# Last output rows in 384 and 128 columns, middle tiles stored in two parts, last load of w_out in two: a two-layer kernel on one core

## The chip, the core and the metric

One core of a Trainium2 chip. The metric is device time in microseconds (us), the median over several executions. All executions here were fast (granted TensorE clock 0.997 to 1.000). A profile is one of these executions; its span is some 2.1 us shorter than the device time of the same execution (285.6 against 287.74 for the kernel before).

## The reference, cut to what matters

```python
kv  = einsum('bhsd,bhse->bhde', k, v)            # 8 batches, 8 heads, 576 rows, 64 wide
out = einsum('bhsd,bhde->bhse', q, kv)
x   = out / sqrt(mean(out*out) + 1e-6) * g_norm  # -> 4608 rows of 512
h   = x @ w_in                                   # 512 -> 2048
y   = (h * sigmoid(1.702 * h)) @ w_out           # 2048 -> 512
```

The kernel works in nine tiles of 512 rows: tiles 0 to 7 hold the first 512 rows of a batch each, tile 8 the 64 rows left over of each of the eight. A tile has a first layer (`hT`, 64 matmuls of 512 columns) and a second layer (`o`, 64 more); the attention of the next batch is woven in between. Step n of a second layer is its n-th matmul, counted from 0.

## The kernel before: the parts that matter

```python
LAST = ((0, DM // 2), (DM // 2, DM))          # DM = 512: two parts of 256 columns

def project_last(mo):                          # tile 8, its last 128 rows
    for i, (n0, n1) in enumerate(LAST):
        o = ps_a.tile([P, n1 - n0], F32, name="oh", tag="att")
        for fo in range(FO):                   # FO = 16 blocks of w_out
            nc.tensor.matmul(o, gT[:, fo, mo * P : (mo + 1) * P],
                             w_out_sb[:, fo, n0:n1], ...)
        copy = nc.vector.tensor_copy if i else nc.scalar.copy
        copy(osb[:, mo, n0:n1], o)
        store_rest(mo, n0, n1)                 # 64 rows on SP's queue, 64 on ACT's

# second layer of tile 0 ("deep"): four passes over four blocks of w_out each
steps = [(mo, 4 * i + k) for i in range(4) for mo in range(4) for k in range(4)]

# loads of w_out, issued by POOL among those of k and v of batch 1
load_w_out(0, 4) ... load_w_out(4, 8)
for c in (0, 2):
    load_half("k", 1, c, c + 2)
    load_half("v", 1, c, c + 2)
    load_w_out(8 + 2 * c, 12 + 2 * c)          # blocks 8-11, then 12-15

# tiles 2 to 7: one store of 1 MB at the end of the tile
nc.sync.dma_start(out=out[t * S : t * S + SM, :].rearrange("(p j) m -> p j m", j=J), in_=osb)
```

## Time and profile before

| | before |
|---|---|
| device time, median | 287.84 us (287.82 to 288.01, 3 executions) |
| TensorE busy | 98% of the span of 285.6 us |
| second layer of tile 0 starts | 28.62 us |
| hole at its step 48 (first use of block 12 of w_out) | 0.27 us |
| last matmul ends | 281.64 us |
| last store issued, seen as landed by SP, end of span | 282.13, 284.38, 285.60 us |

How to read the profile: TensorE does the matmuls; DVE is VectorE, ACT ScalarE, POOL GpSimd, SP SyncE, which here only issues transfers and waits. The page is the overview of one profile; the chain is the work that ended last, followed back from the end. In the chain and the timeline the first column is the start in us, the second the duration; `PE` is a matmul, `PEld` a load of weights, `SPq`, `ACTq`, `POOLq` the queue in which that engine issues. A bracket `[0.39 <-x]` says how long the engine idled before and what ended it. First, what the weight loads of TensorE waited for up to the start of the second layer (total us, times, longest):

```profile
PEld L438 <- DMA w_in_sb<-in_moe_w_in_dram: 0.5, 2, 0.3
```

Second, the traffic and the waits of SP at the very end. The traffic from 281 to 286 us in 40 slices of 0.125 us (DMA share in tenths, then GB/s):

```profile
DMA  3002799940000000006799610000000000000000
GB/s 131 0 0 66 180 221 263 221 99 0 0 0 0 0 0 0 0 8 172 180 238 279 139 33 0 0 0 0 0 0 0 0 0 0 0 0 0 0 0 0
```

The first lump is the store of the first 256 columns, the second that of the last 256. The waits of SP's queue there:

```profile
SPq L710 <- DMA out_dram<-osb: 1.6, 1, 1.6
SPq L498 <- DVE osb L513: 1.3, 1, 1.3
```

L710 is the end of the program: SP waits there 1.6 us for the last store.

### The profile page before, as it was taken

The numbers are of one execution on the slowest core, as the hardware profiler recorded it, in microseconds if no ns is written. First come the engines' busy times: TensorE is split into PE (matmuls) and PEld (weight loads), VectorE is DVE, ScalarE is ACT, GpSimd is POOL, SyncE is SP. The second block draws the span as 40 slices with busy tenths as digits, with TensorE's granted clock in tenths as the row PEclk, the third lists the DMA queues.
The fourth block names the chain that finished last, engine by engine and source line by source line (L and its number), as shares of the span: only waits on it lengthen the run. The fifth ranks groups of instructions, "written<-read, shape, count | busy, mean of one in ns | idle before, by whom it ended". The sixth has DMA issues, their size and how long they took to land.

```text
span 285.6 us, 4343 instructions
## 1 busy us (share of the span) xinstructions
PE 278.9 (98%) x1717; PEld 135.4 (47%) x1717; DVE 119.3 (42%) x233; ACT 156.1 (55%) x273; POOL 56.0 (20%) x78
## 2 busy tenths in 40 slices
PE   7899999999999999999999999999999999999994
PEld 2444544455445544554455445544454444444443
DVE  2540656527651757156713862286327400110011
ACT  2697349766565646574558436762666375026400
POOL 8931541111211121112011401140002000000000
PEclk9999999999999999999999999999999999999999
DMA  8999999995589339963698269924501220021022
GB/s 175 204 205 205 206 251 238 234 268 103 123 166 254 58 73 197 252 116 73 191 197 176 37 186 171 228 54 147 119 2 37 73 112 0 0 92 57 0 73 73
DMA packets 53349, 38.76 MB, mean 136 GB/s; under 512 B 31138, under 2 KB 50850, under 8 KB 52562
## 3 DMA queue, kind: packets, MB, share of 16 engines
q0 software_dynamic: 14944, 15.58, 32.7%
q1 hardware_dynamic: 37664, 21.94, 31.0%
q10 hardware_dynamic: 722, 0.97, 1.2%
q8 instruction: 13, 0.21, 0.3%
q14 instruction: 6, 0.05, 0.0%
HBM read 36.73 MB, written 9.44 MB: 162 GB/s over the span
## 4 chain that ended last, share of the span: by engine, by line
PE 85%; DMA 11%; ACT 1%; POOL 1%; DVE 0%; issue 0%
PE o L475 39%; PE hT L438 39%; DMA w_out_sb<-in_moe_w_out_dram 10%; PE kvp L227 2%; PE outR L291 2%; DMA qf<-in_q_dram 2%; PE oh L505 1%; PE ss L339 1%; PE idle L554 0%; PE q L393 0%; POOL vbuf L112 0%; PE outT L259 0%; ACT qraw L545 0%; PE outT L270 0%; POOL qraw L91 0%
## 5 line engine op out<-in xcount | busy, mean ns | idle before, releaser
L475 PE MATMUL o<-w_out_sb,gT 128*128 128x512 f16 x560 | 130.9, 379 | 0.1
L447 ACT ACTIVATE gT<-hT 128x512 f16<-128x512 f32 x144 | 84.5, 599 | 76.5 <-PE hT L438 76.4
L438 PE MATMUL hT<-xT,w_in_sb 128*128 128x512 f16 x512 | 116.2, 379 | 0.0
L438 PEld LDWEIGHTS <-w_in_sb 128*128 128x128 f16 x576 | 54.5, 98 | 62.3 <-DMA w_in_sb<-in_moe_w_in_dram 0.5
L475 PEld LDWEIGHTS <-gT 128*128 128x128 f16 x560 | 52.8, 98 | 56.5 <-issue 0.7
L485 DVE COPY osb<-o 128x512 f32<-128x512 f32 x20 | 13.8, 691 | 62.3 <-PE o L475 62.3
L323 POOL TENSOR_TENSOR x<-xr,g_all 128x512 f16<-128x512 f32 x12 | 15.3, 1272 | 71.2 <-DVE xr L316 47.2
L218 DVE COPY kpad<-kraw 64x576 f16<-64x576 f16 x56 | 25.0, 446 | 2.0 <-DMA kraw<-in_k_dram 0.7
L302 DVE TENSOR_REDUCE sum<-sq 128x8 f32<-128x512 f16 x24 | 15.8, 679 | 19.9 <-ACT sq L299 19.9
L240 DVE CAST kvb<-kvp 64x128 f16<-64x128 f32 x28 | 8.1, 288 | 36.5 <-PE kvp L227 36.3
L316 DVE TENSOR_TENSOR xr<-outR,sum 128x512 f32<-128x512 f32 x24 | 15.5, 686 | 11.1 <-ACT sum L313 11.1
L112 POOL DMA_DIRECT2D kraw<-in_k_dram x16 | 9.9, 624 | 49.4 <-DVE kpad L218 43.5
L112 POOL DMA_DIRECT2D vbuf<-in_v_dram x16 | 9.7, 608 | 34.0 <-PE kvp L227 29.3
L323 DVE TENSOR_TENSOR x<-xr,g_all 128x512 f16<-128x512 f32 x12 | 15.2, 1268 | 0.7
L299 ACT ACTIVATE sq<-outR 128x512 f16<-128x512 f32 x24 | 13.6, 590 | 2.0 <-PE outR L291 1.6
L227 PEld LDWEIGHTS <-kpad 128*128 128x128 f16 x252 | 11.0, 98 | 7.0 <-DVE kpad L218 0.9
L438 PE MATMUL hT<-x_rem,w_in_sb 128*128 128x512 f16 x64 | 14.0, 379 | 0.0
L279 ACT ACTIVATE sq<-outT 128x512 f16<-128x512 f32 (+1 forms) x16 | 7.7, 481 | 10.5 <-PE outT L259 9.1
L485 ACT COPY osb<-o 128x512 f32<-128x512 f32 x15 | 8.7, 581 | 6.3 <-DMA out_dram<-osb 6.3
L227 PE MATMUL kvp<-vbuf,kpad 128*128 128x64 f16 x252 | 11.9, 193 | 0.1
L312 ACT ACTIVATE sum<-sum,eps_t 128x16 f32<-128x16 f32 x12 | 3.7, 308 | 15.0 <-DVE sum L302 15.0
L341 ACT ACTIVATE ln<-ss,eps_t 128x512 f32<-128x512 f32 (+1 forms) x16 | 9.4, 584 | 4.2 <-PE ss L339 4.1
(62 smaller groups left out, 140.8 us busy)
## 6 DMA issues: line engine op xcount, KB each, us to landing
out_dram<-osb SPq DMA_DIRECT2D x6, 1024.0 KB, 4.3
qf<-in_q_dram SPq DMA_DIRECT2D x5, 1024.0 KB, 8.4
kraw<-in_k_dram POOLq DMA_DIRECT2D x12, 288.0 KB, 5.9
vbuf<-in_v_dram POOLq DMA_DIRECT2D x12, 288.0 KB, 6.1
w_out_sb<-in_moe_w_out_dram POOLq DMA_DIRECT2D x4, 512.0 KB, 14.1
out_dram<-osb SPq DMA_DIRECT2D x6, 192.0 KB, 5.6
qf<-in_q_dram POOLq DMA_DIRECT2D x1, 1024.0 KB, 12.7
kraw<-in_k_dram POOLq DMA_DIRECT2D x7, 144.0 KB, 9.5
```

Of the source, the lines that this page charges most:

```text
L112: nc.gpsimd.dma_start(out=raw[n][l * PH : (l + 1) * PH, c0:c1, 0 : NH * D], in_=srcs[n][b].rearrange("(c l) (p j) d -> l p c (j d)", l=2, ...
L218: nc.vector.tensor_copy(out=kpad[r, c, :, l * D : (l + 1) * D], in_=kraw[r, c, 0 : NH * D].rearrange("p (j d) -> p j d", j=NH),)
L227: nc.tensor.matmul(self.kvp[:, c, :], kpad[:, c, j, :], vbuf[:, c, j * D : (j + 1) * D], start=(j == 0), stop=(j == NH - 1),)
L299: nc.scalar.activation(sq, t, AFT.Square)
L302: nc.vector.tensor_reduce(out=self.sum2[:, j % 2, :], in_=sq.rearrange("p (h d) -> p h d", h=H), op=ALU.add, axis=mybir.AxisListType.X,)
L316: nc.vector.tensor_mul(xr[:, i], self.o[j + i].rearrange("p (h d) -> p h d", h=H), s2[:, i, :].unsqueeze(2).to_broadcast([P, H, D]),)
L323: (nc.vector if i else nc.gpsimd).tensor_mul(self.x16[:, j + i, :].rearrange("p (h d) -> p h d", h=H), xr[:, i], g_all.unsqueeze(1).to_bro ...
L341: nc.scalar.activation(ln[:, 0:n], t[:, 0:n], AFT.Ln, bias=eps_t, scale=1.0 / D)
L438: nc.tensor.matmul(self.h[fo], w_in_sb[:, ko, fo * P : (fo + 1) * P], self.x[:, ko], start=(ko == 0), stop=(ko == KO - 1),)
L447: nc.scalar.activation(self.gT[:, fo, :], self.h[fo], AFT.Gelu_apprx_sigmoid)
L475: nc.tensor.matmul(os[mo], gT[:, fo, mo * P : (mo + 1) * P], w_out_sb[:, fo, :], start=(fo == 0), stop=(fo == FO - 1),)
L485: copy(osb[:, mo, :], os[mo])
```

## The change

The intent: less to copy and store after the last matmul; no burst of 1 MB at the end of a tile; and no waiting for the whole last load of w_out when the first two of its four blocks would do. Cut to its core:

```diff
-    LAST = ((0, DM // 2), (DM // 2, DM))
+    LAST = ((0, 3 * P), (3 * P, DM))
@@ after the copy of row block mo of a tile
+                elif t in HALVED and mo % 2:
+                    store(t, mo - 1, mo + 1)
@@ second layer of tile 0
-            steps = [(mo, 4 * i + k) for i in range(4) for mo in range(4) for k in range(4)]
+            steps = [(mo, 4 * i + k) for i in range(3) for mo in range(4) for k in range(4)]
+            steps += [(mo, f + k) for f in (12, 14) for mo in range(2) for k in range(2)]
+            steps += [(mo, 12 + k) for mo in (2, 3) for k in range(4)]
@@ end of a tile
-        elif t < B:
-            nc.sync.dma_start(out=..., in_=osb)
+        elif t < B and t not in HALVED:
+            store(t, 0, J)
@@ loads of w_out
-        load_w_out(8 + 2 * c, 12 + 2 * c)
+        if c == 0:
+            load_w_out(8, 12)
+        else:
+            load_w_out(12, 14)
+            load_w_out(14, FO)
@@
+    HALVED = (2, 3, 4, 5)
```

`store(t, j0, j1)` is new: it stores the row blocks j0 to j1 - 1 of tile t.

More of the change, by code (lines that the diff above doesn't have):

```diff
@@ L466, in dense @@
                 u()
-        osb = opool.tile([P, 4, DM], F32, name="osb", tag="osb")
+        osb = osbs[t] = opool.tile([P, 4, DM], F32, name="osb", tag="osb")
         os = {}
@@ L536, in dense, with store @@
                 n += m
-        elif t < B:
-            nc.sync.dma_start(
-                out=out[t * S : t * S + SM, :].rearrange("(p j) m -> p j m", j=J), in_=osb
-            )
+        elif t < B and t not in HALVED:
+            store(t, 0, J)
+    def store(t, j0, j1):
+        nc.sync.dma_start(
+            out=out[t * S : t * S + SM, :].rearrange("(p j) m -> p j m", j=J)[:, j0:j1],
+            in_=osbs[t][:, j0:j1],
+        )
     a0 = First(0)
@@ L616 @@
         load_half("v", 1, c, c + 2)
-        load_w_out(8 + 2 * c, 12 + 2 * c)
+        if c == 0:
[3 more added lines that the diff above has]
+            load_w_out(14, FO)
     load_q(2, nc.gpsimd)
     nc.gpsimd.dma_start(out=g_all, in_=g_norm.unsqueeze(0).to_broadcast([P, D]))
+    osbs = {}
+    HALVED = (2, 3, 4, 5)
     live = {0: a0}
```

## The prediction

> **What bounds the kernel now.** I read the page first (shares by engine), then the chain that ended last in order of time, then the waits of TensorE, and then the timeline at the two places where the diff touches something that TensorE waits for.
>
> The page:
>
> ```profile
> span 285.6 us, 4343 instructions
> PE 278.9 (98%) x1717; PEld 135.4 (47%) x1717; DVE 119.3 (42%) x233; ACT 156.1 (55%) x273; POOL 56.0 (20%) x78
> PEclk9999999999999999999999999999999999999999
> ```
>
> TensorE is busy 98% of the span at full clock, and no other engine is past 55%. A busy TensorE need not be at its peak, so I checked the pace: in the chain 64 matmuls of 512 columns take 13.81 us, 215.8 ns each, and the four shapes below agree with each other per column.
>
> ```profile
> 226.35 13.81 PE hT L438 x64
> 240.16 13.81 PE o L475 x64
> 253.97 13.81 PE hT L438 x64
> 267.79 10.36 PE o L475 x48
> 278.15 3.51 PE oh L505 x32
> 281.65 0.02 issue
> 281.68 0.42 DVE osb L513
> ```
>
> From 47.09 us on the chain is TensorE to 281.65 us; after that come one copy, the last store and the close. The five middle tiles repeat with starts at 77.23, 107.06, 136.88, 166.71, 196.52, 226.35: periods of 29.81 to 29.83 us. The last of them (from 196.52) moves 73 GB/s where the others move 140 to 153, and takes 29.83 us as they do. So middle traffic, stores included, does not show in the time. Before 47 us one wait of TensorE is on a transfer of w_out:
>
> ```profile
> 33.04 9.53 DMA w_out_sb<-in_moe_w_out_dram
> 42.57 0.04 issue
> 42.61 0.81 PE o L475 x3
> ```
>
> The chain names this transfer 9.6% of the span, which is not what it costs: TensorE works beside it. What it costs is the hole in the row of weight loads just there:
>
> ```profile
> 42.13 0.10 PEld L475 LDWEIGHTS <-gT 128*128 128x128 f16 x1
> 42.61 0.31 PEld L475 LDWEIGHTS <-gT 128*128 128x128 f16 x2 [0.39 <-issue]
> ```
>
> The matmul at 42.13 is step 47 of the second layer of tile 0; step 48 is the first with block 12 of w_out. At the pace of 0.216 us it would start at 42.13 + 0.22 = 42.35; it starts at 42.61. **The stall is 0.26 us.**
>
> **What the Trainium skill says.** (1) "TensorE: Matmul & The Clock Gate", section "Wait — 56ns, not 53.3ns?": warm matmuls start every N/2.4 GHz plus about 2.5 ns, 215.7 ns at N = 512. The trace agrees: 215.8. It also has four matmuls of 128 columns in 0.22 us (54 to 55 ns each) and nine of 64 columns in 0.26 us (29 ns), so the loads of weights, shown as 98 ns, do not bound even short matmuls here. (2) "VectorE: DVE Perf Modes", section "Why PSUM operands drop a tier": an fp32 copy out of PSUM runs at 1x. In the trace 128x512 took 691 ns and 128x256 425 ns: 266 ns per 256 columns, 1.04 ns a column, which is 1x at 0.96 GHz. (3) "DMA: Bandwidth & Descriptors", section "Anatomy of one DMA — SWDGE (gpsimd) path": some 2 us fixed, mostly the receipt of the write, plus bytes. The stores here issue on other queues, but look alike: 64 KB land in 1.9 (SP) and 2.2 us (ACT), 128 KB in 2.4 and 2.7. (4) Same page, "Specifications": descriptors of at least 512 B for full rate. The new last part has rows of 128 x 4 B = 512 B, just at that line; no transfer of the kernel before shows what such rows do.
>
> **The change, part by part.**
>
> *a. The last load of w_out in two, with the steps to match.* Before, one load brought blocks 12 to 15 and landed at 42.57. After, blocks 12-13 and 14-15 come apart; step 48 needs 12, and block 14 is first needed at step 52 instead of 50. The loads of this stretch run one behind the other on one queue at some 205 GB/s of landed bytes (DMA share 9 tenths throughout). 512 KB take 2.56 us; the first half is done 1.27 us sooner, so it lands at about 41.3 (my estimate), 1.05 us before 42.35. The second lands at about 42.6. Step 52 comes four steps and one 512-column outT matmul after step 48: 42.35 + 5 x 0.216 = 43.43, 0.8 us after that. Both waits vanish and the stall of 0.26 us goes. It can yield no more than that. Since everything behind it to 281.65 is TensorE, all 0.26 should reach the end. Cost: one more issue on POOL, between 0.6 and 0.76 us. POOL idles 0.57 us ahead of the issue at 35.28 and 1.72 us ahead of that at 37.64, waiting for old transfers, and the queue ahead holds data to about 40.8, so the queue doesn't run dry. The copy of row block 0 comes two steps later (step 53 in place of 51), 0.43 us; DVE has room there.
>
> *b. Middle tiles (2 to 5) stored in two parts.* Four more stores. No bytes more, no engine work more, and the period of a tile doesn't feel its traffic (above). 0 us.
>
> *c. The last rows: 384 and 128 columns in place of 256 and 256.* TensorE: 16 x (256 + 256) columns before, 16 x (384 + 128) after. By the formula in (1) that is 16 x (162.5 + 55.8) = 3.49 us against 3.51 measured: 0. The last copy (DVE) shrinks from 425 to 425 - 128 x 1.04 = 292 ns: **-0.13 us**. The copy of the first part grows from 372 to 372 + 128 x 0.81 = 476 ns on ACT (0.81 from 580 and 372 ns), and starts later, at 278.15 + 16 x 0.1625 + 0.03 = 280.78; it ends at 281.25, before TensorE does. Last stores: before, 2 x 64 KB issued at 282.13:
>
> ```profile
> 281.68 0.42 DVE L513 COPY osb<-oh 128x256 f32<-128x256 f32 x1 [2.80 <-PE oh L505]
> 282.13 0.47 SPq L498 DMA_DIRECT2D out_dram<-osb  x1
> 282.13 0.50 ACTq L498 DMA_DIRECT2D out_dram<-osb  x1
> ```
>
> After, 2 x 32 KB at 282.00. Halving the bytes from 128 to 64 KB cut the landing by 0.5 us; at the same slope 64 to 32 KB would cut 0.25. But the 2 x 96 KB of the first part, issued at 281.28, begin to move some 1.4 us later (the lag that the traffic of the last stores shows) and take 0.9 us at 220 GB/s, to about 283.5, and the last part begins at about 283.4: they touch. With that and the short rows I take half of the 0.25: **-0.12 us**.
>
> Sum: 0.26 + 0 + 0.13 + 0.12 = 0.51 us, from 287.84 to **287.35 us** (0.18%).
>
> **The rivals.**
>
> 1. *The wait for w_out only moves to block 14, or the first half lands late.* For it: the load's data seems to be over near 40.8 while its completion comes at 42.57; if that 1.8 us is one slow engine of sixteen with a backlog, the half may land less than 1.27 us sooner. Against: a lead of only 0.22 us is enough. If it came true, the stall stays: 287.6.
>
> 2. *The added store meets the second transpose of x.* SP issues in program order: the half store comes behind the transpose of rows 2 and 3, issued at 103.32 in tile 2's period and landing 3.1 us later, at 106.4; TensorE reads the result at 106.9. Margin 0.5 us. The store would issue at 104.6 and its data move from about 106.0, when the transpose's traffic (104.3 to 105.8) is over. If it did delay the transpose by more than 0.5 us, four tiles would pay a few tenths each: 288.0 to 288.5. I think this unlikely, 1 in 12.
>
> 3. *The tail gives nothing or costs.* If the last part queues fully behind the 192 KB of the first, or rows of 512 B move as slowly as rows of 1 KB, the landing shortens by nothing, and only the copy's 0.13 us remains: 287.45. If the first part's stores hold the queue longer than I think, even that goes: 287.6.
>
> 4. *More from the loads than the stall.* If the earlier traffic shortened other holes before 47 us (0.36 and 0.58 us before the kvp weight loads at 35.4 and 36.4), the gain would be larger, 287.0. But those wait for DVE's kpad copies of blocks already landed, not for w_out.
>
> **Range and chances.** Sure terms are small: 0.26 with a chance of about 8 in 10, 0.13 nearly sure, 0.12 give or take 0.12. The three runs before spread over 0.19 us. That gives 287.0 to 287.7 as the range. A move of 2% is 5.8 us; nothing in the change reaches a tenth of it, either way.
>
> **What would show it.** In the profile after: the hole of 0.39 us in the weight loads at step 48 gone, none at step 52, and the period from there on 29.8 us per middle tile; the start of the last rows near 277.9 in place of 278.15; last matmul near 281.4; a last copy of 0.29 us; the last stores landing in about 1.8 and 2.05 us; four more store issues and one more w_out load. Wrong would be: a wait on w_out at step 52, or a new idle before the first matmuls of tiles 3 to 6 ended by the transpose of x, or a landing above 2.2 us for the last store.

## The result, and the profile after

287.25 us (286.99 to 287.55, 4 executions) against 287.83 (287.82 to 288.01, 4 executions). The ratio is 0.9979, 95% interval 0.9961 to 0.9996. A ratio here is the mean time of one kernel's fast runs over that of the other's of the same rounds, so not quite the ratio of the medians. The predicted 287.35 is 0.1 us off. But the profiled execution, 286.99 us, gained 0.85 us on the median before, and the prediction accounts for 0.51. The lines that answer to those of before, first the page:

```profile
span 284.8 us, 4352 instructions
PE 278.8 (98%) x1717; PEld 134.8 (47%) x1717; DVE 119.2 (42%) x233; ACT 156.1 (55%) x273; POOL 56.7 (20%) x79
```

TensorE is the bound as before. The chain that ended last, its end:

```profile
226.12 13.81 PE hT L438 x64
239.94 13.81 PE o L475 x64
253.75 13.81 PE hT L438 x64
267.56 10.36 PE o L475 x48
277.92 3.51 PE oh L507 x32
281.43 0.02 issue
281.45 0.29 DVE osb L515
```

Every piece comes 0.22 to 0.23 us earlier than before, the 32 last matmuls take 3.51 us as before, and the last copy 0.29 in place of 0.42. The weight loads at step 48, from the timeline:

```profile
41.96 0.75 PEld L475 LDWEIGHTS <-gT 128*128 128x128 f16 x4
42.83 0.10 PEld L259 LDWEIGHTS <-kvb 128*128 128x128 f16 x1
```

The hole is gone: four loads (steps 47 to 50) follow one another at the matmuls' pace; before, 0.39 us of idle stood between those of steps 48 and 49 (a load runs one step ahead of its matmul: the load of step 49 started at 42.61, with the matmul of step 48, and it was this matmul that waited). The chain before had `DMA w_out_sb` for 9.53 us up to that point; the chain after has none of w_out. The two halves of the load landed 8.2 us after 33.17 and 8.8 us after 33.90, at 41.4 and 42.7. The page's row of stores:

```profile
out_dram<-osb SPq DMA_DIRECT2D x8, 512.0 KB, 2.9
out_dram<-osb SPq DMA_DIRECT2D x2, 1024.0 KB, 3.9
```

The eight half stores land in a median of 2.9 us (2.6 to 3.2 each), the 1 MB stores before in 4.3. It is no help to the tiles: their periods are 29.81 to 29.83 us, as before. The end of the program, traffic from 281 to 285 us in slices of 0.1 us:

```profile
DMA  0000000000024998699755750000000000000000
GB/s 0 0 0 0 0 0 0 0 0 0 0 61 138 261 215 169 154 354 369 231 159 144 200 149 21 0 0 0 0 0 0 0 0 0 0 0 0 0 0 0
```

The two lumps have become one: the last part follows hard on the first, as the prediction feared in part, and ends at 283.5. The waits of SP's queue:

```profile
SPq L500 <- ACT osb L515: 1.8, 1, 1.8
SPq L724 <- DMA out_dram<-osb: 1.2, 2, 0.9
```

From the last bytes (283.5) to the end of the span is 1.35 us; before, from 284.0, it was 1.6. Something after the last store became shorter too, and the prediction has no term for it. The records of SP's own instructions at the end of the program show what. Each line is an instruction of SP that waits for two semaphores (start in us; a semaphore is a counter that a finished transfer or engine raises; 107, 109, 112, 113, 114, 116, 117 and 118 are those of the transfers on the SP and ACT queues):

```
before: last stores signal 113 (SP) and 112 (ACT)   after: last stores signal 118 (SP) and 117 (ACT)
282.642  106, 105                                    282.285  106, 105
282.711  107, 104                                    282.355  107, 104
282.772  109, 103                                    282.416  109, 103
284.375  112, 102   <- the last store                282.480  112, 102
284.437  113, 101                                    282.542  113, 101
284.496  114, 100                                    283.481  114, 100   <- the first part's store
284.557  116,  99                                    283.543  116,  99
284.617  117, 108                                    283.870  117, 108   <- the last store
284.678  118, 115                                    283.931  118, 115
285.595  end of span                                 284.848  end of span
```

The program's closing runs through nine such instructions, in a fixed order, some 61 ns each. The eight transfer semaphores are taken in turn by the transfers of the two queues. Which of them the last pair of stores gets depends on how many transfers the whole program has issued there: four stores more moved the pair from the fourth and fifth instruction to the eighth and ninth. So after the last landing five instructions remained before and one remains after: 4 x 61 ns = 0.24 us. From landing to end: 1.22 us before, 0.98 after.

That theory, and the rest of the account, were then tested.

### The profile page after: what moved, and what is told of

Its sections match the earlier page's. It is cut to its first block, busy times and chain, and to the rows that moved or that the text cites. A ratio compares the mean times of both kernels' runs of the same rounds, so it can differ in the third digit from the quotient of the medians.

```text
span 284.8 us, 4352 instructions
## 1 busy us (share of the span) xinstructions
PE 278.8 (98%) x1717; PEld 134.8 (47%) x1717; DVE 119.2 (42%) x233; ACT 156.1 (55%) x273; POOL 56.7 (20%) x79
## 4 chain that ended last, share of the span: by engine, by line
PE 93%; POOL 2%; DMA 2%; DVE 1%; issue 0%; POOLq 0%
PE hT L438 44%; PE o L475 42%; PE kvp L227 3%; DMA vbuf<-in_v_dram 2%; PE outR L291 2%; PE oh L507 1%; PE ss L339 1%; POOL qraw L91 1%; POOL kraw L91 1%; DVE kpad L218 1%; POOL vbuf L91 1%; PE outT L259 0%; PE q L416 0%; PE outT L270 0%; PE idle L562 0%
## 5 line engine op out<-in xcount | busy, mean ns | idle before, releaser
L112 POOL DMA_DIRECT2D kraw<-in_k_dram x16 | 9.9, 623 | 48.3 <-DVE kpad L218 42.6
```

Source lines behind the costliest of these rows:

```text
L112: nc.gpsimd.dma_start(out=raw[n][l * PH : (l + 1) * PH, c0:c1, 0 : NH * D], in_=srcs[n][b].rearrange("(c l) (p j) d -> l p c (j d)", l=2, ...
```

## The experiments

Eleven kernels ran, five executions each, all with correct results. Kernels are compared only within the same rounds. The edits are shown against the kernel named.

The five times of one kernel spread over 0.1 to 0.7 us, as much as the effects. Of e1 to e11 only e7 and e8, which hold the whole change, have an interval of the ratio to before that excludes 1; the others are unclear by their times alone, so the profiles decide. The table holds for each profile: when the second layer of tile 0 starts; the hole in the weight loads at step 48 beyond the pace of 0.216 us; issue to landing of the last store; how many waits of SP follow it; landing to end; the span less the start of the second layer, which takes out what happens before it; and the mean device time less that of before. "Late" kernels carry an extra matmul.

| kernel | 2nd layer starts | hole | store lands in | waits left | landing to end | span - start | mean time - before |
|---|---|---|---|---|---|---|---|
| before | 28.62 | 0.27 | 2.25 | 5 | 1.22 | 256.98 | |
| after | 28.67 | 0 | 2.10 | 1 | 0.98 | 256.18 | -0.62 |
| e1 loads and steps | 28.90 | 0 | 2.26 | 5 | 1.22 | 256.72 | -0.14 |
| e2 split load, old steps | 29.03 | 0 | 2.23 | 5 | 1.22 | 256.70 | -0.02 |
| e3 tail | 29.20 | 0.03 | 2.17 | 5 | 1.22 | 256.51 | -0.16 |
| e4 halves | 28.63 | 0.28 | 2.22 | 1 | 0.98 | 256.73 | -0.29 |
| e5 four idle loads | 28.98 | 0.05 | 2.22 | 1 | 0.97 | 256.51 | -0.27 |
| e6 before, late | 29.21 | 0 | 2.26 | 5 | 1.22 | 256.73 | +0.14 |
| e7 after, late | 28.74 | 0 | 2.09 | 1 | 0.98 | 256.18 | -0.54 |
| e8 after again | 28.81 | 0 | 2.15 | 1 | 0.97 | 256.26 | -0.61 |
| e9 three parts | 29.01 | 0 | 2.07 | 1 | 0.97 | 256.21 | -0.30 |
| e10 after without halves | 29.14 | 0 | 2.17 | 5 | 1.22 | 256.50 | -0.18 |
| e11 six idle loads | 28.54 | 0.48 | 2.22 | 7 | 1.35 | 257.28 | +0.18 |

### e1: the loads and the steps alone

Edit on the kernel before: the two hunks of the diff on `steps` and on the loads of w_out.

> Part a alone (w_out in two loads and the new order of steps). The prediction's own step: the stall of 0.26 us at step 48 goes and nothing else changes: last matmul 0.26 to 0.28 us earlier against the start of the second layer, time -0.26 us against before (287.57). If the loads are worth more than the stall, below -0.4; if the wait only moves to block 14, within 0.05 of before. Issues on the SP and ACT queues are as many as before, so after the last store has landed the closing still runs through 5 more semaphore waits of SP (1.22 us from the landing to the end, as before).

Measured: 287.72 us median, mean 0.14 below before; ratio 0.9995, interval 0.9983 to 1.0008. The hole is gone, the closing is as before, as expected. The gain is about half of what was expected. The profiled execution's second layer starts at 28.90, not 28.62, and a late start leaves less of a hole to gain (below); the starts of the other four executions are not on record.

### e2: the split load with the old steps

Edit on the kernel before: the hunk on the loads alone.

```diff
-        load_w_out(8 + 2 * c, 12 + 2 * c)
+        if c == 0:
+            load_w_out(8, 12)
+        else:
+            load_w_out(12, 14)
+            load_w_out(14, FO)
```

> The split load with the old order of steps. In the changed kernel the halves landed at 41.4 and 42.7 us; with the old order block 14 is needed at step 50, which would come at about 42.8. If the split does the work: -0.2 to -0.28 us, hole at step 48 gone, at most 0.1 us at step 50. If the order of steps does the work: a wait of 0.2 us or more moves to step 50 and the gain is under 0.1 us.

Measured: 287.85 us, mean 0.02 below before, interval of the ratio 0.9987 to 1.0012. No hole at step 48 and none at step 50; but the second layer started at 29.03, so block 14 was asked for 0.4 us later than in a prompt execution. Span less start is 256.70, that of e1 is 256.72. In this execution the new order of steps does nothing; whether it does in a prompt one, where the margin would be about 0.1 us, this run doesn't show.

### e3: the tail alone

Edit on the kernel before: the hunk on `LAST`.

> Part c alone (384 and 128 columns). The prediction's step: -0.13 us for the copy and -0.12 us for the landing, -0.25 together. By my reading of the two traces the changed kernel also gained 0.24 us after its last store had landed, because SP at the end waits on the store semaphores one by one (61 ns each) in a fixed order, and four more stores move the last store from the fourth wait to the eighth of nine. If so, e3, which adds no store, keeps 5 waits after the last landing and gains only 0.25 to 0.29; rival: the shorter closing comes from the smaller last store, then e3 gains about 0.5.

Measured: 287.66 us, mean 0.16 below before, less than the 0.25 to 0.29 expected; interval 0.9982 to 1.0007. The copy took 0.29 us, the last store landed 2.17 us after its issue, 5 waits and 1.22 us followed. The rival (a smaller last store shortens the closing) is out. The hole at step 48 is down to 0.03 us without any edit there, because the second layer started at 29.20. The waits of the weight loads up to that point:

```profile
PEld L438 <- DMA w_in_sb<-in_moe_w_in_dram: 1.8, 4, 0.6
```

1.8 us of waiting for w_in, where the profile of before had 0.5. Nothing was edited there.

### e4: the halved stores alone

Edit on the kernel before: the hunks on `store` and `HALVED`.

> Part b alone (four middle tiles stored in two parts). The prediction said 0 us. The closing theory says: last matmul where it was before, last store landing as before, but only 1 wait of SP after it in place of 5: -0.24 us, with 0.98 us from the landing to the end in place of 1.22. Rival: the stores slow a transpose of x and the periods of tiles 3 to 6 grow past 29.83 us.

Measured: 287.61 us, mean 0.29 below before; interval 0.9978 to 1.0005. The chain up to the last copy, from the first full tile on:

```profile
47.11 9.62 PE hT L438 x44
77.26 8.63 PE hT L438 x40
...
278.18 3.51 PE oh L507 x32
```

TensorE runs as in the kernel before (47.09 and 278.15 there), the hole at step 48 is there (0.28), the last store lands in 2.22 us. All of the gain lies after the landing: 0.98 us against 1.22. The prediction's 0 for this part is wrong, and its reason (traffic of middle tiles doesn't show) is right.

### e5: four loads that nothing reads

Edit on the kernel before:

```diff
+        if t == 6:
+            for i in range(4):
+                extra = const.tile([1, D], F32, name=f"extra{i}")
+                at1(9, lambda e=extra: nc.sync.dma_start(out=e, in_=g_norm.unsqueeze(0)))
```

> The kernel before with four loads of 256 B each on SP's queue in tile 6, that nothing reads: no store is halved, only the count of transfers on the two hardware queues is 4 larger. Theory (the closing runs through the store semaphores in a fixed order, eight of them taken in turn): the last store's semaphore moves four places to the end, 1 wait of SP follows its landing in place of 5, landing to end 0.98 us in place of 1.22, time -0.24 us as with the halved stores. Rival (the halved stores themselves helped): 1.22 us and no change.

Measured: 287.60 us, mean 0.27 below before; interval 0.9978 to 1.0003. One wait left, 0.97 us from landing to end. Four useless loads of 256 B give what the halved stores gave.

### e6 and e7: a late start, with and without the wait for w_out

The same edit, for e6 on the kernel before and for e7 on the changed kernel:

```diff
                 self.h[fo] = (pool or ps_h).tile([P, SM], F32, name="hT", tag=tag)
+                if self.t == 0 and fo == FO - 1:
+                    nc.tensor.matmul(self.h[fo], w_in_sb[:, ko, fo * P : (fo + 1) * P],
+                                     self.x[:, ko], start=True, stop=True)
```

> The kernel before with one matmul of 512 columns more (0.216 us), its result overwritten, at the end of tile 0's first layer, so that the second layer starts that much later. Theory: the wait for w_out at step 48 ends at a time set by the transfers, so it takes up a late start as long as the start is less than 0.26 us late; the hole shrinks from 0.26 to about 0.04 us and the time stays within 0.05 us of before, in executions that started early; in those that started late by themselves it grows by up to 0.216. Rival: the late start shifts everything, +0.22 us.

> The changed kernel with the same extra matmul. It has no wait at step 48 any more, so nothing takes the late start up: +0.22 us against the changed kernel in the same call (e8), near 287.5. If the wait were not what takes it up, e6 and e7 would move by the same amount.

Measured: e6 +0.14 us against before, e7 +0.07 against e8 (means 287.36 and 287.29). The theory wanted about 0 and +0.22; the times go, if anywhere, the other way, and with executions that spread over half a microsecond (e7: 287.03 to 287.70) they decide nothing. The profiles fell badly too: e6's execution had started late by itself (29.21 - 0.216 = 28.99), e7's early (28.74 - 0.216 = 28.52). What e6 does show is that at a start of 29.21 the kernel with the whole load has no hole at all:

```profile
42.29 0.10 PEld L339 LDWEIGHTS <-ones 128*128 128x128 f16 x1
42.51 0.74 PEld L483 LDWEIGHTS <-gT 128*128 128x128 f16 x4
```

### e8: the changed kernel again

> The changed kernel once more, for the spread of its times and as the partner of e7. Theory: its times spread by as much as the start of its second layer does (28.6 to 29.2 us in the six profiles so far), so between 287.0 and 287.6, median near 287.3; the profile's start of the second layer, plus 249.25 us, gives the end of TensorE's work (281.42 - 28.67 = 252.75 to the last matmul in the first profile), and the span follows it to within 0.1 us.

Measured: 287.38 us median (287.06 to 287.43), mean 0.61 below before, ratio 0.9979, interval 0.9966 to 0.9991: the result repeats. (The 249.25 in the expectation is a slip; the 252.75 behind it is the figure.) Its profile starts the second layer at 28.81; 28.81 + 252.75 = 281.56, and the last matmul ended at 281.59.

### e9: the last rows in three parts

Edit on the changed kernel:

```diff
-    LAST = ((0, 3 * P), (3 * P, DM))
+    LAST = ((0, 2 * P), (2 * P, 3 * P), (3 * P, DM))
-    HALVED = (2, 3, 4, 5)
+    HALVED = (2, 3)
```

> The changed kernel with the last rows in three parts (256, 128, 128 columns) and only tiles 2 and 3 halved, so that the two stores more of the tail and the two fewer of the middle leave the last store's semaphore where the changed kernel has it. Theory: last copy 0.29 us as there, the last store has less ahead of it and lands in 2.0 to 2.1 us instead of 2.10 and 2.15, 16 more short matmuls cost 0.04 us: within 0.1 us of the changed kernel, 287.2 to 287.4. Rival: the 192 KB of the first part do hold the last store up, then it gains 0.2 us.

Measured: 287.52 us, mean 0.30 below before, out of the expected range. The last store lands in 2.07 us, where the two profiles of the changed kernel have 2.10 and 2.15. Span less start is 256.21 against 256.18 and 256.26: from there on the profile is that of the changed kernel, in an execution that started at 29.01. Why the mean of five lies 0.3 us above the changed kernel's is not shown beyond that: the other four starts are not on record. No better version was found; the changed kernel is the fastest of those that ran.

### e10: the changed kernel without the halved stores

Edit on the changed kernel:

```diff
-    HALVED = (2, 3, 4, 5)
+    HALVED = ()
```

> The changed kernel without part b (all middle tiles stored in one). Theory: 5 waits of SP after the last landing again, 1.22 us from landing to end, time +0.24 us against the changed kernel: 287.5. The prediction on record, by which part b is worth 0, says no change (287.3).

Measured: 287.77 us (287.17 to 287.86), mean 0.18 below before. 5 waits, 1.22 us. Span less start 256.50, 0.24 to 0.32 more than in the profiles of the changed kernel (after, e8) and its late twin (e7); 0.24 of it is the closing. The mean gain is 0.43 us smaller than the changed kernel's, more than the 0.24 expected; the profiled execution also started late, at 29.14. Interval of the ratio to before: 0.9981 to 1.0006.

### e11: six idle loads

Edit: e5 with `range(6)`.

> The kernel before with six unread loads of 256 B instead of four. Eight semaphores taken in turn: the last pair of stores moves six places on, which is two back, to the second wait of the nine: 7 waits after the landing, 1.34 us from landing to end in place of 1.22, +0.12 us against before. Rival (more transfers are better for some other reason): 1.0 us or less from landing to end.

Measured: 288.02 us, mean 0.18 above before (interval of the ratio 0.9993 to 1.002). The last pair signals the second and third instruction's semaphores, 7 waits follow, 1.35 us from landing to end. More transfers make it worse, exactly where the count says so. This execution started earliest of those with the whole load, and its hole is the longest:

```profile
42.74 0.10 PEld L475 LDWEIGHTS <-gT 128*128 128x128 f16 x1 [0.59 <-issue]
```

## Why the prediction was right, point by point, and where it was not

**The total (287.35 against 287.25) is right, and the sum under it is partly so by luck.** Its three terms were 0.26, 0 and 0.25 us.

**Part a, the load and the steps: mechanism right, term too large.** The prediction read one hole of 0.26 us in one profile and let all of it reach the end. The hole is not a constant. Over the six profiles with the whole load it falls, but for 0.01 us, as the start of the second layer gets later: 28.54: 0.48; 28.62: 0.27; 28.63: 0.28; 28.98: 0.05; 29.20: 0.03; 29.21: 0. In the five with a hole, step 48 begins 0.04 us after the load has landed; in e6 the load landed at 42.77 and step 48 came only at 42.94. So the wait ends when the transfer lands, and a late start uses it up. The landing moves too, from 42.57 to 42.92 over these six, but less than the start. In all seven profiles with the split load it is 0. So the gain of part a is the mean of what the hole would have been: about 0.2 us over the five that have no matmul added ((0.48 + 0.27 + 0.28 + 0.05 + 0.03) / 5 = 0.22), and 0.14 by the times of e1. The landing of the first half was sized well (41.3 predicted, 41.4 measured; second 42.6 and 42.7), rival 1 did not come true. Nor did rival 4, more from the loads than the stall: e1's span less start is 0.26 us below that of before (256.72 against 256.98), no more than the hole.

A late start goes with the first layer of tile 0 waiting for w_in: the waits total 0.3 to 0.7 us in the profiles that start by 28.67 and 1.4 to 1.8 in those that start from 28.81 on (e7, at 28.74 with its added matmul, has 0.2). The landing records of the traces settle it. The last of the five loads of w_in brings blocks 10 to 15, 24 matmuls or 5.18 us of work, and lands between 23.01 and 23.97. In the nine profiles where it lands at 23.43 or later, the second layer starts 5.24 us after that landing in every one (in e6 after taking off the added matmul); in the other four it starts 5.30 to 5.52 us after (e7 too without its added matmul). So this load sets the start in those nine. Why it lands sooner in some executions than in others is open; the edits don't touch it.

**Part b, the halved stores: the step "No bytes more, no engine work more ... 0 us" failed.** What it says of the tiles held (periods 29.81 to 29.83). What it left out is that four transfers more turn the semaphores on by four, which takes 0.24 us out of the closing. e4 (1 wait left, -0.29 us mean), e5 (the same with four idle loads, -0.27), e10 (5 waits again) and e11 (7 waits, +0.18) settle this: it is the count of transfers and not the size of the stores. The waits left and the time from landing to end show it, the means only agree. Rival 2, a transpose of x delayed by a half store, is out: in the changed kernel these transposes still land in 3.1 us (3.2 us the longest in its first profile), and the periods have not grown.

**Part c, the tail: right in its terms.** The copy: 0.13 predicted, 425 to 292 ns measured. The landing: 0.12 predicted; the mean from issue to landing is 2.24 us over the seven profiles with 256 columns last (before, e1, e2, e4, e5, e6, e11) and 2.13 over the five with 384 and 128 (after, e3, e7, e8, e10), 0.10 less. Together 0.23; e10 less e1 and e2 in span less start gives 0.20 to 0.22. The 192 KB ahead do touch the last part, as the traffic shows, and e9, which takes a third of them away from it, lands at 2.07: it costs under 0.1 us. The prediction misread one figure here: it lets bytes move 1.4 us after the issue, but the stores issued at 282.13 move theirs from 283.25 on (the second lump above), 1.1 us after. As the lag holds for both parts, their order and the touching come out the same. That half of 0.25 was left of the landing was a guess; it came out at 0.10.

The sum as measured in profiles: some 0.2 (a, by execution 0 to 0.5) + 0.24 (b) + 0.23 (c) = 0.67 us; by times 0.61 and 0.62. With e1, e4 and e3 alone the means give 0.14 + 0.29 + 0.16 = 0.59, but the interval of each of these three includes no change, so this sum by itself proves little; the parts rest on the profiles.

## What to carry to other kernels

A wait for a transfer is worth what is left of it in the mean execution, not what one profile shows: look at several profiles, and at how early the waiting engine got there. Where a program's time is compared at a tenth of a per cent, count what follows the last landing: the semaphore that the last store happens to get, and with it the time to the end (0.97 to 1.35 us in these runs), depends here on the number of transfers issued on two queues in the whole program, and an edit that adds or removes some can move it. Subtracting the start of the steady part from the span takes the scatter of the first loads out of such a comparison, except where a later wait, as that at step 48, takes part of it up.

## What the Trainium skill lacked or had wrong

- "Runtime: NRT & Kernel Launch", section "The ~15µs preamble/postamble breakdown", lists a barrier of about 1.5 us after the kernel, which no run here shows apart, but no page says that part of what follows the last landing depends on which semaphore the last store has. In these runs 1, 5 and 7 waits of about 61 ns followed it, and landing to end took 0.97 to 0.98, 1.22 and 1.35 us.
- "DMA: Bandwidth & Descriptors", section "Anatomy of one DMA — SWDGE (gpsimd) path", splits the time of a transfer issued by POOL into a fixed part of about 2 us and one by bytes. The last rows' stores are issued by SP and ACT, always as a pair, and are near it at small sizes: 64 KB in rows of 1 KB landed in 1.9 and 2.2 us and 32 KB in rows of 512 B in 1.9 and 2.1. From 64 to 128 KB they took 0.5 us more (2.4 and 2.7), where the page's rate would give 0.15 us (an estimate: 64 KB at 436 GB/s) for one alone and 0.3 us for the pair. The page gives no scatter between executions: the last load of w_in landed 12.4 to 13.2 us after its issue, and with it the start of the second layer moved by 0.67 us (28.535 to 29.203, kernels without an added matmul).
